# A hybrid of window attention and mixture-of-experts attention: another order of all engines, and matmuls that nobody reads in the first part

## The chip, the cores and the metric

The kernel runs on 1 core of one Trainium2 chip. The metric is the device time in microseconds; the time of the kernel before is the median of 3 runs. TensorE (PE) multiplies into PSUM, VectorE (DVE), ScalarE (ACT) and GpSimd (POOL) do the rest, and SyncE (SP) issues nearly all DMAs. Each engine takes its instructions strictly in the order in which they were laid.

## The reference

```python
def _attn_ref(q, k, v):                      # q, k, v: 8 x 8 heads x 576 x 64
    scores = scale * np.matmul(q, k.transpose(0, 1, 3, 2))
    mask = (rel >= 0) & (rel < 64)           # rel = query position - key position
    attn = softmax of scores where mask
    return np.matmul(attn, v)

def _moe_ref(x, w_gate, wq, wk, wv, wo):     # x: 8 x 576 x 512, the heads side by side
    logits = x @ w_gate                      # 4 experts; the best 2 are weighted by a softmax
    for e in range(4):
        q, k, v = x @ wq[e], x @ wk[e], x @ wv[e]            # 64 wide
        a = softmax of causal scale * (q @ k.T)
        ye = a @ v @ wo[e]
        out += weight of e for each row * ye
```

## The kernel before

The work is one program of units. A unit is a Python generator that issues some instructions at each step, and the table `ORDER` lists the units' names in the order in which their next steps are issued; behind a colon stand the PSUM banks that the step takes. The order of `ORDER` is the order of every engine's queue. There is no other scheduler.

Stage 1 is the window attention, in 72 groups `g` (9 for each batch). `p` loads q and k of two pairs of heads, `h` the values into one of three `vt` tiles. `m` makes scores of two groups (L324), `q` is their softmax (L336 to L377, over VectorE, GpSimd and ScalarE), `t` transposes the probabilities by a product with `ident` (L390) and multiplies them by the triangle masks (L393), `a` multiplies them with the values (L415) and splits the result into a high and a low f16 half, `xh` and `xl` (L440, L442). All stage 1 products are fp32.

Stage 2 is the attention of the experts, by batch: `v`, `k`, `r` (the q of stage 2) are projections of `xh` and `xl` by split weights (L566 to L568), each followed by its own split (`kt`, `qt`). `x` makes scores, `y` masks them with the running minimum (L696) and takes exp (L700), `u` weights and splits them (L732 to L755), `D` transposes them by DMA (L764), `A` multiplies them with the values (L797), `o` is the output product. `g` is the gate.

`w` prepares the weights once: the largest absolute value (L257), spread over the partitions by a product with `fours` (L262), its inverse (L265, L267), and the split. `n` takes the largest absolute value of a batch's `vt` tiles (L458, 1280 columns), `M` turns it into the scale `sc` of that batch through two small products (L465, L470) and L473, L474.

At the start `f` clears a tile `px` and issues seven matmuls of it (L209) that nobody reads. In the last batch `IDLE` puts such matmuls between the products of `A`.

Of the kernel before, what the change touches and what calls it, by code (L numbers as in the profile page):

```python
# [143 lines left out]
def window_attention_moe_attention(ctx: ExitStack, tc: tile.TileContext, qT, kT, vW,  # L144
# [10 lines left out]
    def bank():  # L155
        return PS[:, banks.pop(0)]
# [339 lines left out]
    M2 = {}  # L496
# [312 lines left out]
    def s2_o(b, j):  # L809
# [20 lines left out]
        else:  # L830
            for i in range(2):
                (nc.scalar if ends and i else nc.sync).dma_start(out[b - 1 + i, 512:576], t[64 * i:64 * i + 64])


    units = {}

    def unit(name, f, *args):
# [107 lines left out]
```

## Time and profile before

| | |
|---|---|
| median of 3 runs | 438.84 us (436.96 to 441.39) |
| time of the profiled execution | 440.07 us |
| its span | 438.4 us |
| mean granted clock of TensorE | 0.978 |
| PE busy | 390.5 us (89%), 5885 matmul records |
| DVE busy | 343.1 us (78%) |
| ACT busy | 327.4 us (75%) |
| POOL busy | 299.1 us (68%) |
| DMA moved | 71.79 MB, mean 164 GB/s |

The span is the time from the first to the last instruction of the profiled execution. An engine is busy while one of its instructions runs; a matmul's end is modelled, and matmuls overlap. Idle time of TensorE is shown with what ended it. One fp32 matmul of L209, L262, L324 or L415 leaves two records.

### The profile page before, as it was taken

What the parts mean: (1) busy time and instruction counts of PE and PEld (TensorE: products, weight loads), DVE (VectorE), ACT (ScalarE), POOL (GpSimd) and SP (SyncE); (2) the same over time, 40 slices, a digit from 0 to 9 for tenths busy, and PEclk for the clock granted to TensorE, in tenths of its full rate; (3) what the DMA queues carried; (4) which work ended last, traced back from release to release, by engine and by line L of the source; (5) the groups of instructions that cost most, each with busy time, mean ns of one, the idle gap of its engine ahead of it and who ended that gap; (6) DMA issues with size and microseconds to landing.
All of it is one profiled execution on the core that took longest, in us unless ns stands there. A gap on an engine that the chain in (4) does not pass through costs nothing. (4 is left out here: it accounts for less than half of the span.)

```text
span 438.4 us, 15501 instructions
## 1 busy us (share of the span) xinstructions
PE 390.5 (89%) x5885; PEld 296.4 (68%) x5885; DVE 343.1 (78%) x1043; ACT 327.4 (75%) x1143; POOL 299.1 (68%) x669
## 2 busy tenths in 40 slices
PE   4567998997989899999989989999999999989885
PEld 4556777776776676776676766677767775767573
DVE  2878899979897568979869877888878777878830
ACT  0756657887989577885997878967888759969942
POOL 7477533598899884887878888587699866484200
PEclk9768999999999999999999999999999999999998
DMA  7950504399299993879589968986469834587993
GB/s 247 333 187 33 201 28 137 137 187 210 62 236 209 202 242 131 191 125 187 106 200 231 221 91 161 281 178 156 91 126 203 117 63 114 116 161 128 192 229 102
DMA packets 145114, 71.79 MB, mean 164 GB/s; under 512 B 126224, under 2 KB 128784, under 8 KB 145040
## 3 DMA queue, kind: packets, MB, share of 16 engines
q1 hardware_dynamic: 144960, 70.68, 72.9%
q8 instruction: 46, 0.75, 0.8%
q14 instruction: 28, 0.23, 0.2%
q10 hardware_dynamic: 80, 0.13, 0.1%
HBM read 30.94 MB, written 9.44 MB: 92 GB/s over the span
## 5 line engine op out<-in xcount | busy, mean ns | idle before, releaser
L755 POOL TENSOR_TENSOR sp<-p,sp 128x320 f16<-128x320 f32 (+3 forms) x110 | 100.7, 915 | 9.2
L700 ACT ACTIVATE p<-p,r 128x320 f32<-128x320 f32 (+3 forms) x128 | 77.4, 609 | 16.2 <-DVE r L696 15.6
L744 ACT ACTIVATE sp<-p,r 128x192 f16<-128x192 f32 (+3 forms) x128 | 76.5, 616 | 1.8 <-DVE r L736 1.3
L754 POOL TENSOR_SCALAR p<-p,r 128x320 f32<-128x320 f32 (+3 forms) x110 | 64.5, 586 | 17.9 <-ACT sp L744 16.1
L352 ACT ACTIVATE p<-ps,st 128x64 f32<-128x64 f32 x204 | 61.4, 318 | 13.1 <-POOL st L349 11.8
L696 DVE CUSTOM_DVE_ANT_0 p<-ps,causal,sc 128x320 f32<-128x320 f32 (+2 forms) x128 | 63.6, 543 | 2.3 <-PE ps L685 1.9
L324 PE MATMUL ps<-k,q 64*64 64x128 f32 (+1 forms) x1152 | 45.1, 290 | 7.0 <-DMA k<-in_kT_dram 3.5
L377 POOL TENSOR_TENSOR p<-p,st 128x256 f32<-128x256 f32 x72 | 43.4, 614 | 8.3 <-DVE st L373 3.8
L393 DVE TENSOR_TENSOR pt<-ps,tri 128x1024 f32<-128x1024 f32 (+1 forms) x40 | 44.2, 1109 | 3.6 <-PE ps L390 3.3
L797 PE MATMUL ps<-tu,v 128*64 128x64 f16 (+2 forms) x1056 | 41.2, 229 | 5.4 <-DMA tu<-sp 2.7
L324 PEld LDWEIGHTS ps<-k,q 64*64 64x64 f32 x1152 | 36.9, 146 | 13.2 <-issue 3.2
L797 PEld LDWEIGHTS <-v 128*64 128x64 f16 x1056 | 37.4, 111 | 10.1 <-issue 8.1
L352 ACT ACTIVATION_READ_ACCUMULATOR p<-ps,st 128x1 f32 x204 | 43.0, 211 | 0.0
L685 PE MATMUL ps<-kt,qt 64*128 64x320 f16 (+3 forms) x480 | 39.8, 292 | 3.4 <-DVE pt L393 0.9
L415 PE MATMUL ps<-pt,vt 64*64 64x128 f32 (+1 forms) x1440 | 40.9, 250 | 1.8 <-DVE xl L442 0.7
L415 PEld LDWEIGHTS ps<-pt,vt 64*64 64x64 f32 x1440 | 36.3, 134 | 7.3 <-issue 1.6
L566 PE MATMUL ps<-xh,wkhi 128*128 128x256 f16 (+1 forms) x128 | 36.6, 286 | 2.9 <-DVE sc L473 1.8
L566 PE MATMUL ps<-xh,wqhi 128*128 128x256 f16 (+1 forms) x128 | 36.6, 286 | 1.6 <-ACT p L352 0.7
L566 PE MATMUL ps<-wvhi,xh 128*128 128x260 f16 x128 | 35.5, 277 | 2.0 <-DVE pt L393 1.4
L567 PE MATMUL ps<-xl,wkhi 128*128 128x256 f16 (+1 forms) x128 | 36.6, 286 | 0.2 <-DVE xl L442 0.2
L568 PE MATMUL ps<-xh,wqlo 128*128 128x256 f16 (+1 forms) x128 | 36.6, 286 | 0.0
L567 PE MATMUL ps<-xl,wqhi 128*128 128x256 f16 (+1 forms) x128 | 36.6, 286 | 0.0
(152 smaller groups left out, 1002.2 us busy)
## 6 DMA issues: line engine op xcount, KB each, us to landing
vt<-in_vW_dram SPq DMA_DIRECT2D x16, 576.0 KB, 5.5
out_dram<-out SPq DMA_DIRECT2D x32, 256.0 KB, 3.1
q<-in_qT_dram SPq DMA_DIRECT2D x14, 576.0 KB, 4.6
k<-in_kT_dram SPq DMA_DIRECT2D x14, 576.0 KB, 6.2
tu<-sp SPq DMA_TRANSPOSE x96, 3.9
out_dram<-out SPq DMA_DIRECT2D x7, 128.0 KB, 2.8
q<-in_qT_dram SPq DMA_DIRECT2D x2, 320.0 KB, 7.3
k<-in_kT_dram SPq DMA_DIRECT2D x2, 320.0 KB, 7.0
```

The costliest lines, as they stand in the source:

```text
L324: nc.tensor.matmul(S1[g][o:o + 64, i, c:], lhsT=q_t[r, i % 2, 64 * b:64 * b + 64], rhs=k_t[r, i % 2, 64 * b + c - 64:64 * b + 64], start=T ...
L352: nc.scalar.activation(pt[:, i], ps[:, i, 64:128], AF.Exp, bias=st[:, 0, z + i:z + i + 1], scale=0.125, accum_out=st[:, 1, z + i:z + i + 1])
L393: nc.vector.tensor_tensor(t, ps[:, :, None].to_broadcast([128, n, 2, 128]), tri[:, None].to_broadcast([128, n, 2, 128]), op=OP.mult)
L415: nc.tensor.matmul(to, lhsT=values[d][r, h, b + e - (w == 0)], rhs=rhs, start=(e, h) not in started, stop=s == n - 1, skip_group_check=True)
L566: nc.tensor.matmul(ps, lhsT=ah, rhs=bh, start=first, stop=False)
L567: nc.tensor.matmul(ps, lhsT=ah, rhs=bl, start=False, stop=False)
L696: nc.vector.tensor_tensor_reduce(out=dst, in0=src, in1=mask, scale=SC[b][:, 3:4], scalar=above, op0=OP.add, op1=OP.min, accum_out=to)
L700: nc.scalar.activation(p, p, AF.Exp, bias=r2[:, 0, x:x + 1], scale=-1.0, accum_out=r2[:, 1, x:x + 1])
L744: nc.scalar.activation(hi, p, AF.Copy, scale=by)
L754: nc.gpsimd.tensor_scalar(p, p, by, 1.0, op0=OP.mult, op1=OP.mult)
L755: nc.gpsimd.tensor_tensor(lo, p, hi, op=OP.subtract)
L797: nc.tensor.matmul(to, lhsT=V2[b % 2][:, c, a, 2 * pr + h], rhs=rhs, start=n == 0, stop=n == len(work_list) - 1, skip_group_check=True)
```

## The change

`ORDER` is replaced as a whole. It has the same units and steps, in another order and with other banks, and seven new ones named `F`. The durations by which the new order was laid were measured for each kind of instruction; they don't stand in the kernel. A unit `F<a or b><n>_<count>` issues `count` fp32 matmuls of 128x128 by 128 columns into a bank that the order gives it, with `px` (a) or `ident` (b) as both operands; nobody reads the result.

```diff
 ORDER = (
-    'c p0 h0 e0 p1 f:0 i h1 l0 l1 p0 n0 p1 d e1 l2 z l3 m0:01 h2 m2:23 q0 q1 q0 q3 q0 q1 q0 q2 q1 n0 q1 q1 q0 w0 q1 '
...
+    'i h0 f:0 c p0 p1 l0 h1 l1 p0 z p1 n0 l2 l3 Fa0_13:1 m0:01 h2 m2:23 q0 d q1 e1 q0 e0 q3 q0 q1 q0 w0 q1 q0 q1 q2 '
+    'Fb1_9:4 w0:0 q1 n0 q1 q1 q2 q1 q3 w0 q1 w0 Fb2_8:4 t1:0 n0 q3 w1 q2 M0:1 q2 w0 M0 Fb3_3:4 w1:4 t1 q3 M0 m8:5 q3 '
...
+    def keep_busy(n, of):
+        ps = bank()[:, :128]
+        for _ in range(n):
+            nc.tensor.matmul(ps, lhsT=of, rhs=of, start=True, stop=True)
...
             x, _, y = x.partition(":")
+            if x[0] == "F":
+                unit(x, keep_busy, int(x[1:].split("_")[1]), PX[0].rearrange("r a c -> r (a c)") if x[1] == "a" else ident)
             banks[:] = map(int, y)
             next(units[x], None)
```

The counts are 13, 9, 8, 3, 6, 3 and 4, 46 in all; the last stands ahead of t3. All other lines move down by one, so that L390 is L391 after the change.

Three places follow. The first is TensorE's queue from the weight factors of `v` (L262) to the scores m8. Before:

```order
L262 MATMUL ps<-largest,fours 128x1 x2
L390 MATMUL ps<-ident,p_0_253 128x128 x2
L390 MATMUL ps<-ident,p_1_257 128x128 x2
L465 MATMUL ps<-ident,mv_187 1x128
L262 MATMUL ps<-largest,fours 128x1
L470 MATMUL ps<-m_0_304,one 128x1
L324 MATMUL ps<-k_137,q_136 64x128 x4
```

And the same part of TensorE's queue now; L839 is the new line:

```order
L839 MATMUL ps<-ident 128x128 x9
L263 MATMUL ps<-largest,fours 128x1 x2
L839 MATMUL ps<-ident 128x128 x8
L391 MATMUL ps<-ident,p_0_265 128x128 x2
L391 MATMUL ps<-ident,p_1_270 128x128 x2
L466 MATMUL ps<-ident,mv_204 1x128
L839 MATMUL ps<-ident 128x128 x3
L263 MATMUL ps<-largest,fours 128x1
L471 MATMUL ps<-m_0_334,one 128x1
L325 MATMUL ps<-k_172,q_171 64x128 x4
```

The work that is read stands in the same order; 9, 8 and 3 unread matmuls stand ahead of the factors of `v`, of t1 and of the factor of `k`. The other 13 of the start stand right behind the seven of L209, and 6, 3 and 4 follow behind the scores.

The second place is VectorE's queue around the scale of batch 2 (`sc_1581`, from M2) and the maximum over the values of batch 3 (`mv_1563`, from n3). Before:

```order
L592 SCALAR_TENSOR_TENSOR v_1_113<-ps,v_1_113 128x256
L458 TENSOR_REDUCE mv_1563<-vt_84 128x1
L592 SCALAR_TENSOR_TENSOR v_0_114<-ps,v_0_114 64x256
L473 TENSOR_SCALAR sc_1581<-ps 128x1
L474 RECIPROCAL sc_1581<-sc_1581 128x1
```

The same place of VectorE's queue now, where the scale is called `sc_1591` and the maximum `mv_1611`:

```order
L474 TENSOR_SCALAR sc_1591<-ps 128x1
L475 RECIPROCAL sc_1591<-sc_1591 128x1
L340 COPY_PREDICATED ps<-win,ps 128x4x64
L459 TENSOR_REDUCE mv_1611<-vt_84 128x1
L807 SCALAR_TENSOR_TENSOR y_105<-ps,y_105 128x320
L593 SCALAR_TENSOR_TENSOR v_1_113<-ps,v_1_113 128x256
L652 SCALAR_TENSOR_TENSOR qt_103<-ps,qt_103 128x256
```

The scale stood behind the maximum and now stands ahead of it; a y part, a value part and a query part stand behind it.

The third place is VectorE's queue around the first maximum of batch 4 (`mv_2477`, over `vt_86`) and the second half of the keys `kt_116` of batch 2. Before:

```order
L651 SCALAR_TENSOR_TENSOR kt_115<-ps,kt_115 128x256
L651 SCALAR_TENSOR_TENSOR qt_103<-ps,qt_103 128x256
L458 TENSOR_REDUCE mv_2477<-vt_86 128x1
L393 TENSOR_TENSOR pt_30_2497<-ps,tri 128x1024
L347 TENSOR_REDUCE st_33_2516<-ps 128x4
L651 SCALAR_TENSOR_TENSOR kt_116<-ps,kt_116 128x256
```

The same place of VectorE's queue now, where the maximum is called `mv_2667`:

```order
L394 TENSOR_TENSOR pt_30_2652<-ps,tri 128x1024
L652 SCALAR_TENSOR_TENSOR kt_116<-ps,kt_116 128x256
L459 TENSOR_REDUCE mv_2667<-vt_86 128x1
L652 SCALAR_TENSOR_TENSOR qt_104<-ps,qt_104 128x320
L348 TENSOR_REDUCE st_33_2611<-ps 128x4
```

The triangle multiply and the keys stood behind the maximum and now stand ahead of it.

## Rows read from the trace of the kernel before

**Rows 1.** Busy us by stretch: length, PE, PEld, DVE, ACT, POOL, clock, DMA.
```profile
9.50:45.00 35.50, 24.63 (x396) 21.32 (x399) 27.31 (x61) 20.54 (x91) 22.48 (x40) 0.76 0.54 185
45.00:100.00 55.00, 51.33 (x826) 39.55 (x823) 50.39 (x140) 40.81 (x168) 30.59 (x80) 1.00 0.53 146
100.00:420.00 320.00, 298.38 (x4525) 223.28 (x4525) 260.40 (x827) 261.38 (x875) 238.26 (x507) 1.00 0.80 162
```

**Rows 2.** Longest waits of PE, 45 to 420 us: total, times, longest.
```profile
PE ps L566 <- DVE sc L473: 1.8, 1, 1.8
PE ps L324 <- DVE kt L651: 1.5, 1, 1.5
PE ps L390 <- DVE v L592: 1.4, 1, 1.4
```

**Rows 3.** The stretch view again, in windows of 2 us (clock third from the end).
```profile
14.00:16.00 2.00, 0.00 (x0) 0.00 (x0) 2.00 (x2) 1.69 (x12) 0.20 (x1) 0.98 1.08 367
...
24.00:26.00 2.00, 2.00 (x44) 2.00 (x40) 1.47 (x5) 0.00 (x0) 0.23 (x2) 0.50 0.00 0
...
28.00:30.00 2.00, 0.35 (x2) 0.30 (x2) 2.00 (x2) 1.86 (x13) 1.73 (x5) 0.89 1.02 369
...
32.00:34.00 2.00, 1.27 (x28) 1.30 (x30) 2.00 (x4) 2.00 (x9) 1.82 (x3) 0.50 0.87 326
```

**Rows 4.** PE's timeline, 0 to 47 us: start, us, what, [idle before <- releaser].
```profile
3.20 3.36 PE L209 MATMUL ps<-px 128*128 128x128 f32 x14 [3.20 <-DVE win L203]
...
9.50 3.19 PE L324 MATMUL ps<-k,q 64*64 64x64 f32 x60 [2.54 <-DMA k<-in_kT_dram]
16.48 0.98 PE L262 MATMUL ps<-largest,fours 128*128 128x1 f32 x4 [3.79 <-DVE largest L257]
18.13 1.09 PE L390 MATMUL ps<-ident,p 128*128 128x128 f32 x4 [0.67 <-POOL st L349]
...
20.45 5.17 PE L324 MATMUL ps<-k,q 64*64 64x128 f32 x78
...
27.56 0.38 PE L262 MATMUL ps<-largest,fours 128*128 128x1 f32 x2 [0.84 <-DVE largest L257]
29.20 0.35 PE L262 MATMUL ps<-largest,fours 128*128 128x1 f32 x2 [1.26 <-DVE largest L257]
30.65 1.09 PE L390 MATMUL ps<-ident,p 128*128 128x128 f32 x4 [1.10 <-DVE inverse L265]
32.73 1.98 PE L324 MATMUL ps<-k,q 64*64 64x64 f32 x32 [0.99 <-DMA k<-in_kT_dram]
...
41.36 0.66 PE L390 MATMUL ps<-ident,p 128*128 128x128 f32 x4
...
46.25 1.10 PE L324 MATMUL ps<-k,q 64*64 64x128 f32 x32
```

**Rows 5.** Timeline of all engines, 0 to 60 us: VectorE's rows, one load issue.
```profile
0.90 0.17 DVE L533 MEMSET m_f<- 128x128 f32 x1 [0.90 <-PEq L931]
...
22.47 0.43 DVE L339 COPY_PREDICATED ps<-win,ps 128x256 f32<-128x256 uint32 x1 [1.07 <-PE ps L324]
...
24.18 0.76 DVE L339 COPY_PREDICATED ps<-win,ps 128x256 f32<-128x256 uint32 x2 [1.28 <-PE ps L324]
...
25.88 0.39 SPq L179 DMA_DIRECT2D q<-in_qT_dram  x1
25.95 0.43 DVE L339 COPY_PREDICATED ps<-win,ps 128x256 f32<-128x256 uint32 x1 [0.36 <-PE ps L324]
```

**Rows 6.** The same view at three maxima over loaded values.
```profile
98.10 1.49 DVE L458 TENSOR_REDUCE mv<-vt 128x1 f32<-128x1280 f32 x1 [1.34 <-DMA vt<-in_vW_dram]
...
149.08 1.49 DVE L458 TENSOR_REDUCE mv<-vt 128x1 f32<-128x1280 f32 x1 [1.66 <-DMA vt<-in_vW_dram]
...
337.64 1.49 DVE L458 TENSOR_REDUCE mv<-vt 128x1 f32<-128x1280 f32 x1 [0.76 <-DMA vt<-in_vW_dram]
```

**Rows 7.** One line's durations: ns min/median/max, first and last start, forms.
```profile
L393 DVE TENSOR_TENSOR pt<-ps,tri x40: 681/1215/1225, 19.7 to 375.2; 128x1024 f32<-128x1024 f32 x32, 128x512 f32<-128x512 f32 x8
```

194 rows, old and new, of the table ORDER are left out of this document.

## Prediction

> **What bounds the kernel now.** I read four views in turn. The busy time by stretch [rows 1] shows TensorE as the engine that limits nearly all of the span: from 45 to 420 us it is busy 51.33 + 298.38 = 349.7 of 375 us, so 25.3 us idle in single pieces. VectorE is close behind from 45 to 100 us (50.39 of 55). From 9.5 to 45 us no engine is full: TensorE 24.63 and VectorE 27.31 of 35.5 us, at a mean granted clock of 0.76. That stretch is a chain of waits: first loads, scores, softmax, transposes, weight factors, then the loads of the next pairs.
>
> [...] VectorE waited for TensorE in this slow stretch [rows 5]: 1.07, 1.28 and 0.36 us for scores, while the loads of the next pairs were issued at 25.88, once the last scores of the old pairs were done.
>
> Behind 45 us the longest waits of TensorE [rows 2] are single events of 1.8, 1.5 and 1.4 us, all for VectorE. The timeline [rows 6] names what VectorE did then: it had itself waited 1.34, 1.66 and 0.76 us for a load of values (`vt`), to take that load's maximum (L458, 1.49 us). What TensorE wanted stood behind it.
>
> **Term 1, the faster clock in the first part.** Matmul counts below are records; one fp32 matmul makes two. A full-speed set of scores is 32 records in 1.10 us, 34 ns each at 46.25 [rows 4].
> - The first scores, 60 records in 3.19 us, are 53 ns each. That pace lies between 34 and the 62 ns of the set at 32.73 (1.98 us for 32), so I count them as partly slow: 60 x 19 ns = 1.1 us.
> - The transposes of t1 take 1.09 us at 18.13 and 0.66 at 41.36: 0.4 us.
> - m8, m4 and m6 (80 records) run at 5.17 us for 78, 66 ns each: 80 x 32 ns = 2.6 us. The next loads of q and k are issued when they end, so the scores at 32.73, which waited for such a load (0.99 us), move with them.
>
> Together 4.1 us. t3 (30.65) and m9 (32.73) would shrink by 0.4 and 0.9 as well; VectorE is 77% busy in this stretch and has work of its own there, so I keep that 1.3 for the upper bound, 5.4. The lower bound is nothing: if the clock is not held, or if VectorE's own queue sets the pace. I take **-4.1**.
>
> **Term 2, the unread matmuls themselves.** There are 46, each fp32 of 128x128 and 128 columns. The seven at the start took 3.36 us, 0.48 each [rows 4]. No row shows one at full clock: half of 0.48 is 0.24, and a factor matmul at about full clock, with the same weights and one column, takes 0.35 to 0.38. Thirteen stand ahead of the first scores. With the seven they last 20 x 0.48 = 9.6 us; they begin when VectorE has cleared their operand, at 3.20 before and now as VectorE's second row: its first row starts at 0.90 [rows 5], so about 1.4, an estimate. They end at 11.0 at the slow pace, 1.5 us behind the load that released the scores at 9.50, and before it if the pace doubles on the way. The other 33 cost 15.8 us slow, 12.5 at 0.38 and 7.9 at 0.24. The gaps they are to fill are 3.79 + 0.67 + 0.84 + 1.26 + 1.10 = 7.7 us [rows 4], and 4.1 more if term 1 comes true: 11.8. So at full clock they nearly fit in sum, but not gap by gap: the eight ahead of t1 (1.9 to 3.0 us) meet a gap of 0.67 plus whatever the factor matmuls come earlier. Bounds 0 and +8.2 + 1.5 = +9.7 (slow throughout). The middle of the run should be at full clock, so I take **+1.5**.
>
> **Term 3, the maxima that wait for loads.** In the old order the scale of batch 2 (L473) stood behind the maximum over `vt_84`; the new order has it ahead, and the key part `kt_116`, for which TensorE waited 1.5 us, now stands ahead of the maximum over `vt_86`. Those two stalls go, 1.8 and 1.5 us [rows 2]. At the third (1.4 us) other rows stand behind the maximum, and I can't tell. All three: 4.7. But loads and maxima are no further apart everywhere, and a y part, a value part and a query part now stand behind the two maxima. Each new wait would cost VectorE what the old ones did, 0.76 to 1.66 us, and TensorE about as much. Bounds -4.7 and 0; I take half, **-2.4**.
>
> **Term 4, the rest of TensorE's idle time.** 25.3 - 4.7 = 20.6 us in pieces of about 1 us at most. Every engine's rows move, so each piece may go or another come. For it speaks that one kind takes one time: the triangle multiply of 1024 columns is 1.22 us with median and maximum 10 ns apart [rows 7], so an order laid with measured durations can meet its waits. Against it: nothing shows that the old order's small pieces came from wrong durations. Bounds -10 (half goes) and +6 (a third more). I take a tenth, **-2.0**.
>
> **Sum.** -4.1 + 1.5 - 2.4 - 2.0 = -7.0 us. The profiled execution has a span of 438.4 and a time of 440.07 us, so about 1.7 lie around the span; the median of the three runs is 438.84 (436.96 to 441.39). Against the span that is 431.4, with what lies around it 433.1, against the median **431.8**.
>
> No load, transpose, split, bank count or tile is added or removed, so the queues' bytes are as before. On SyncE's queue the first load is now values instead of q and k; the same loads stand ahead of the second k either way, so I cost that at nothing. The unread matmuls write banks that no live tile uses, so nothing but TensorE's queue pays for them. The end (420 us on) keeps its order: the same products wait for the same transposes, and I cost it at nothing.
>
> **Rivals.**
> - **Bigger gain.** Half of TensorE's 25.3 us idle goes, because each wait was planned with the right duration: -12.6 - 4.1 + 1.5 = -15.2, 423.6 us. For: the idle pieces are small and the durations steady. Against: on the stretch from 100 to 420 all four engines are 74% to 93% busy, which leaves little to move.
> - **No change.** The clock's gain is limited to what VectorE waited for (1.07 + 1.28 + 0.36 = 2.7), the unread matmuls take 1.5 back, and the load waits only move to other maxima: -1.2, 437.6 us. For: VectorE is 92% busy from 45 to 100, so TensorE may run ahead only to wait for it.
> - **Slower: the unread matmuls stand in the way.** They are in TensorE's queue, in front of t1, the factors and the next transposes, and can't be skipped. What stands behind them is released late, and ScalarE, GpSimd and the next loads with it. Slow they cost 15.8 against 7.7 us of gaps, 8.2 too much, and 1.5 at the start; nothing of term 1 comes back. With terms 3 and 4 as taken, 438.8 + 9.7 - 4.4 = 444.1 us. It decides from 0.36 us for one on (11.8 / 33): above it the first part is longer than before. Against: 0.38 was measured with the clock only just up, and 20 in a row at the start leave TensorE busy from 1.4 us.
>
> [...]
>
> **How the numbers follow.** Likeliest (427 to 434.4): 0.42. Bigger gain (under 427): 0.18. No change (434.4 to 443.2): 0.27. [...] One per cent, 4.4 us, is about what a measurement of this kernel can tell from no change: faster 0.60, same 0.27, slower 0.13. For 8 in 10 the range takes in the bigger gain's price and stops short of the slow rival's: 423 to 443. The likeliest case alone has 427 to 434.4.
>
> **What would show it.** Term 1: a granted clock of 1.00 from about 15 to 45 us, m8, m4 and m6 at 34 ns a record, and the loads that were issued at 25.88 issued 3 to 4 us earlier. Term 2: an unread matmul at 0.24 to 0.36 us, and t1 no later than 18.1. Term 3: no wait of TensorE over 1 us for L473's or a `kt` part's sake behind a maximum; VectorE may still wait for a load; it is TensorE's waits that count. Term 4: TensorE idle under 25 us from 45 to 420. I am wrong if the clock is 1.00 and the first part still ends when it did (VectorE bound it), or if it is short and the stretch behind it has grown by as much.

## The result, and the profile after

The changed kernel takes 422.88 us (median of 4 runs, 422.35 to 423.95) beside 438.78 of the kernel before on the same chip: ratio 0.9636, 95% interval 0.9583 to 0.969, 15.9 us faster. I had forecast 431.8 and 423 to 443. The direction was right; the size was more than twice the forecast, and the time lies just outside the range. Its profiled execution has a span of 420.8 us.

The busy time by stretch, as in [rows 1], then the stretch from 145 to 390 us by itself (columns as there; the clock is third from the end):
```profile
9.50:45.00 35.50, 30.19 (x569) 25.73 (x573) 31.62 (x75) 25.19 (x112) 26.33 (x48) 1.00 0.62 220
45.00:100.00 55.00, 50.31 (x782) 39.71 (x774) 48.25 (x139) 38.76 (x150) 31.19 (x75) 1.00 0.57 146
100.00:420.00 320.00, 304.99 (x4593) 228.43 (x4591) 258.83 (x824) 264.83 (x881) 233.79 (x501) 0.99 0.81 168
...
145.00:390.00 245.00, 241.61 (x3698) 182.40 (x3696) 211.22 (x667) 212.02 (x716) 195.50 (x416) 1.00 0.83 169
```
The kernel before in that last stretch:
```profile
145.00:390.00 245.00, 229.34 (x3499) 172.10 (x3499) 195.82 (x612) 195.77 (x672) 187.21 (x406) 1.00 0.79 162
```
Here lies most of the gain: TensorE's idle time falls from 15.7 to 3.4 us, and in the same 245 us it issues 3698 matmul records for 3499, 5.7% more. The first part runs at a clock of 1.00 for 0.76, and from 45 to 100 us TensorE is no busier than before.

TensorE's timeline of the first part, as in [rows 4]:
```profile
1.39 3.36 PE L210 MATMUL ps<-px 128*128 128x128 f32 x14 [1.39 <-DVE px L203]
4.54 3.99 PE L839 MATMUL ps<-px 128*128 128x128 f32 x26
...
9.63 1.76 PE L325 MATMUL ps<-k,q 64*64 64x64 f32 x60 [0.83 <-DMA k<-in_kT_dram]
11.32 2.27 PE L839 MATMUL ps<-ident 128*128 128x128 f32 x18
...
16.73 0.68 PE L391 MATMUL ps<-ident,p 128*128 128x128 f32 x4 [0.38 <-DVE inverse L266]
...
18.73 2.84 PE L325 MATMUL ps<-k,q 64*64 64x128 f32 x80
...
29.22 1.10 PE L325 MATMUL ps<-k,q 64*64 64x64 f32 x32
...
33.03 1.20 PE L325 MATMUL ps<-k,q 64*64 64x128 f32 x32 [1.09 <-DVE pt L394]
...
36.10 1.13 PE L416 MATMUL ps<-pt,vt 64*64 64x64 f32 x48 [1.19 <-DVE p L360]
...
38.67 0.41 PE L391 MATMUL ps<-ident,p 128*128 128x128 f32 x2 [1.44 <-DVE pt L394]
```
L839 are the unread matmuls, two records each: 3.99 / 13 = 0.31 us, later 2.27 / 9 = 0.25. m8, m4 and m6 (18.73) take 35 ns a record for 66. From 33 us on TensorE waits for VectorE.

The table compares places rather than times. Every step of TensorE is weighed with the time that a step of its kind takes in before when nothing holds it up (unread matmuls count nothing), and the sums are lined up: how many us earlier than in before a kernel has done the same work. The columns are times of before. Each row is one execution beside one execution of before, which was itself 1.3 us over its median; so the last column lies above what the medians say (2.2 for 0.4 in old_maxima). In kernels that equal before up to there, or all but, the entry differs from 0 by up to 2.5, so that much is chance. The kernels are told of below; "old" begins from the order of before, "new" from that of after. The median of old_pe leaves out one run that was over 1.5% longer than its fastest.

| kernel | 37 | 92 | 148 | 237 | 325 | 413 | 430 | median us | ratio to before, 95% |
|---|---|---|---|---|---|---|---|---|---|
| after | 6.5 | 3.2 | 3.0 | 7.2 | 14.2 | 21.8 | 17.5 | 422.88 | 0.9636 [0.9583, 0.969] |
| new_no_unread | 0.7 | -4.3 | -3.2 | -0.4 | 5.8 | 13.8 | 9.2 | 426.03 | 0.9741 [0.9677, 0.9804] |
| old_unread | -2.5 | -2.6 | -2.7 | -3.5 | -4.3 | -4.0 | -3.4 | 444.32 | 1.0153 [1.0105, 1.0201] |
| old_unread2 | 3.4 | 3.3 | 3.2 | 2.3 | 1.5 | 2.1 | 2.7 | 438.57 | 1.0003 [0.9976, 1.003] |
| old700_new | 0.6 | -1.0 | -5.9 | -1.1 | 5.9 | 14.2 | 9.0 | 430.28 | 0.9799 [0.9735, 0.9864] |
| new710_old | 6.6 | 3.4 | -0.1 | -6.3 | -7.2 | -6.7 | -6.1 | 444.98 | 1.0145 [1.0104, 1.0186] |
| old_maxima | 1.3 | 0.8 | 0.7 | 1.5 | 1.4 | 2.0 | 2.2 | 437.65 | 0.999 [0.9966, 1.0015] |
| old_banks | 1.0 | -1.3 | -4.7 | -13.7 | -20.1 | -24.0 | -24.1 | 463.19 | 1.0563 [1.0519, 1.0607] |
| old_banks2 | 1.1 | 0.8 | 0.9 | 1.1 | 1.3 | 1.8 | 1.6 | 438.17 | 0.9994 [0.9966, 1.0021] |
| new_banks | 6.5 | 3.1 | 3.1 | 7.1 | 15.7 | 24.4 | 19.1 | 421.42 | 0.9617 [0.9572, 0.9663] |
| old_v | 0.4 | -0.5 | -6.4 | -4.8 | -4.7 | -5.9 | -9.1 | 450.39 | 1.0267 [1.0194, 1.0341] |
| old_pe | 0.0 | 0.0 | -2.8 | -12.3 | -19.3 | -25.1 | -24.7 | 464.58 | 1.0546 [1.0431, 1.066] |
| new_all | 6.5 | 1.1 | -5.6 | -14.0 | -11.5 | -8.4 | -17.6 | 458.44 | 1.0438 [1.0375, 1.0501] |
| old_v2 | 2.5 | 1.6 | 0.8 | -0.2 | 0.8 | 2.7 | -0.3 | 437.32 | 0.9946 [0.9919, 0.9973] |
| old_pe2 | 0.4 | -1.0 | -2.2 | -4.5 | -6.4 | -4.2 | -4.5 | 443.71 | 1.009 [1.006, 1.012] |
| old_all2 | 1.2 | 0.2 | 2.4 | 5.7 | 8.2 | 14.8 | 13.6 | 427.16 | 0.9737 [0.971, 0.9763] |
| new_all2 | 7.0 | 4.5 | 5.5 | 8.8 | 13.6 | 20.8 | 16.0 | 424.51 | 0.9655 [0.9606, 0.9704] |
| new_tail | 6.1 | 3.0 | 2.8 | 7.0 | 15.6 | 22.4 | 19.9 | 422.42 | 0.9624 [0.9584, 0.9664] |

So after gains 6.5 us up to 37, loses 3.5 of them up to 148, gains 18.8 up to 413, and gives 4.3 back at the end.

The loss up to 148 has two places. By the same sums 2 us are gone by 45 us, where TensorE waits for VectorE. Some 3 more go between 110 and 130, where after's clock falls again, from 119 us on, behind idle pieces of 0.99, 0.74 and 0.20 us in which TensorE waited for VectorE:
```profile
116.55 0.58 PE L686 MATMUL ps<-kt,qt 64*128 64x320 f16 x6 [0.99 <-DVE r L697]
117.88 0.74 PE L686 MATMUL ps<-kt,qt 64*128 64x448 f16 x6 [0.74 <-DVE m L697]
```
```profile
118.00:120.00 2.00, 1.80 (x34) 1.30 (x32) 2.00 (x9) 2.00 (x8) 1.92 (x3) 0.78 1.07 121
120.00:122.00 2.00, 2.00 (x48) 2.00 (x43) 1.73 (x5) 1.19 (x6) 1.75 (x4) 0.50 1.42 126
```

### The profile page after: what moved, and what is told of

Its sections match the earlier page's. It is cut to its first block, busy times and chain, and to the rows that moved or that the text cites. A ratio compares the mean times of both kernels' runs of the same rounds, so it can differ in the third digit from the quotient of the medians.

```text
span 420.8 us, 15689 instructions
## 1 busy us (share of the span) xinstructions
PE 392.9 (93%) x5977; PEld 301.0 (72%) x5977; DVE 342.7 (81%) x1043; ACT 328.8 (78%) x1143; POOL 299.1 (71%) x669
## 5 line engine op out<-in xcount | busy, mean ns | idle before, releaser
L755 POOL TENSOR_SCALAR p<-p,r 128x320 f32<-128x320 f32 (+3 forms) x110 | 64.6, 587 | 22.1 <-ACT sp L745 15.7
L745 ACT ACTIVATE sp<-p,r 128x320 f16<-128x320 f32 (+3 forms) x128 | 75.8, 613 | 0.9 <-POOL r L737 0.3
L378 POOL TENSOR_TENSOR p<-p,st 128x256 f32<-128x256 f32 x72 | 43.3, 616 | 14.3 <-DVE st L374 13.5
L798 PE MATMUL ps<-tu,v 128*64 128x256 f16 (+2 forms) x1056 | 41.5, 230 | 3.7 <-DVE y L807 1.7
L325 PE MATMUL ps<-k,q 64*64 64x128 f32 (+1 forms) x1152 | 39.9, 271 | 3.4 <-DVE r L697 1.2
L416 PE MATMUL ps<-pt,vt 64*64 64x128 f32 (+1 forms) x1440 | 39.4, 252 | 2.4 <-DVE p L360 1.2
L416 PEld LDWEIGHTS ps<-pt,vt 64*64 64x64 f32 x1440 | 35.3, 136 | 7.7 <-issue 2.7
L325 PEld LDWEIGHTS ps<-k,q 64*64 64x64 f32 x1152 | 32.6, 134 | 8.5 <-DVE r L697 2.4
L569 PE MATMUL ps<-xh,wklo 128*128 128x256 f16 (+1 forms) x128 | 36.6, 286 | 0.0
```

Of the source, the lines that this page charges most:

```text
L325: nc.tensor.matmul(S1[g][o:o + 64, i, c:], lhsT=q_t[r, i % 2, 64 * b:64 * b + 64], rhs=k_t[r, i % 2, 64 * b + c - 64:64 * b + 64], start=T ...
L416: nc.tensor.matmul(to, lhsT=values[d][r, h, b + e - (w == 0)], rhs=rhs, start=(e, h) not in started, stop=s == n - 1, skip_group_check=True)
L569: nc.tensor.matmul(ps, lhsT=al, rhs=bh, start=False, stop=last)
L745: nc.scalar.activation(hi, p, AF.Copy, scale=by)
L755: nc.gpsimd.tensor_scalar(p, p, by, 1.0, op0=OP.mult, op1=OP.mult)
L798: nc.tensor.matmul(to, lhsT=V2[b % 2][:, c, a, 2 * pr + h], rhs=rhs, start=n == 0, stop=n == len(work_list) - 1, skip_group_check=True)
```

## Experiments on the first part: the unread matmuls

All edits are to `ORDER`. In new_no_unread the seven entries are taken out of after; in old_unread they are put into before at the same places.
```diff
-... Fa0_13:1 m0:01 ... Fb1_9:4 w0:0 ...      after
+... m0:01 ... w0:0 ...                       new_no_unread
...
-... m0:01 ... w0:0 ...                       before
+... Fa0_13:0 m0:01 ... Fb1_9:0 w0:0 ...      old_unread
+... Fa0_13:6 m0:01 ... Fb1_9:7 w0:0 ...      old_unread2
```
new_no_unread: 

> The changed kernel without the 46 unread matmuls. Theory of the prediction: the clock falls again between 15 and 36 us, terms 1 and 2 are lost together (4.1 - 1.5), 425.5 us. Rival 'the gain is in the order behind 145 us': the lead at 145 us is 3.0 us, so at most 426, and 422.5 to 423.5 if the order alone made that lead. If the unread matmuls carried most of the gain: 432 or more.

It is 3.1 us slower than after (426.03), or 4.2 where each is set against the runs of before on its own chip. The sign agrees with the 2.6 of terms 1 and 2; the size is uncertain, since the intervals of the two ratios overlap. This kernel's runs spread over 6.3 us (424.53 to 430.84) where after's spread over 1.6. The execution profiled here is the slowest of the four (430.84, mean granted clock 0.956); the other three took 424.53 to 426.41 at 0.979 to 0.987, and after's four had 0.987 to 0.991. So this trace, and its row in the table, overstate what the unread matmuls are worth. Its clock, by stretch:
```profile
14.00:16.00 2.00, 0.97 (x4) 0.93 (x4) 2.00 (x4) 1.48 (x11) 0.25 (x2) 0.50 1.08 366
24.00:26.00 2.00, 1.66 (x30) 1.26 (x22) 2.00 (x5) 0.76 (x5) 0.70 (x3) 0.55 0.00 0
```
old_unread: 

> The order and the banks of before with the 46 unread matmuls put in at the same seven places (ahead of the first scores, of the factors of v, of t1, of the factors of k, q and o, and of t3). Theory of the prediction: 438.8 - 4.1 + 1.5 = 436.2 us. Rival 'they stand in the way': 440 or more. If they carried most of the gain: 430 or less.

A miss by 8 us; the rival came true. The timeline shows why:
```profile
15.58 4.18 PE L840 MATMUL ps<-ident 128*128 128x128 f32 x18 [3.67 <-ACT p L354]
19.55 0.85 PE L264 MATMUL ps<-largest,fours 128*128 128x1 f32 x4
...
24.55 0.86 PE L392 MATMUL ps<-ident,p 128*128 128x128 f32 x4
```
I had given the nine unread matmuls the bank of the step behind them. They waited 3.67 us for ScalarE, its last reader, filled no gap, and ran at the slow pace (0.46 us each) in front of the factors; t1 came at 24.55 for 18.13. In after they go to banks that nobody reads at that time. So they do in the next kernel.

old_unread2: 

> Before with the 46 unread matmuls at the same seven places as in old_unread, but in banks that nobody reads at that time, so that they need not wait. Prediction's terms 1 and 2: -4.1 + 1.5 = -2.6, 436.2 us; with the bounds of term 2 from 434 to 447. Rival (in the old order they stand in the way even so): over 440, as old_unread's 444.3. Sign of the first: the 78 records of m8, m4 and m6 at 34 to 36 ns each and begun before 20.45; of the second: t1 later than 18.13.


```profile
9.50:45.00 35.50, 29.61 (x557) 25.85 (x557) 28.48 (x68) 23.25 (x102) 24.47 (x45) 1.00 0.54 185
```
```profile
12.46 2.28 PE L840 MATMUL ps<-ident 128*128 128x128 f32 x18
16.89 0.58 PE L264 MATMUL ps<-largest,fours 128*128 128x1 f32 x4 [2.15 <-DVE largest L259]
...
19.19 0.60 PE L392 MATMUL ps<-ident,p 128*128 128x128 f32 x4
...
20.93 2.73 PE L326 MATMUL ps<-k,q 64*64 64x128 f32 x78
```
Full clock throughout, 35 ns a record, t1 1 us late, and 3.4 us ahead at 37 in this trace; the medians show no difference (1.0003, so within about 1.3 us either way). Of the first sign the pace came true and the start did not (20.93, not before 20.45); the second sign came true. The steps in the chain (weight maxima, factors) wait for VectorE, 2.15 us ahead of the first factor, at a clock of 1.00 too. From old_unread to old_unread2 only four bank numbers of unread matmuls differ: 5.8 us, and 1.5% by the ratios.

The executions of before say the same. In the 70 that stand beside these runs the mean granted clock lies anywhere from 0.970 to 0.992. The 19 with 0.985 or more are not faster (in the median 0.3 us above the median of their chip) than the 42 under 0.98 (0.1 below it). So in the old order the time does not hang on the mean clock. The clock of [rows 3] was that of one execution: in old700_new below, whose first part is that of before, it is 0.90 from 9.5 to 45 us for 0.76.

## Experiments on the middle: which part of the order

**Splices.** Up to about 145 us one order, behind it the other.
```diff
+... x113:51 y112 u101 k200 v22:7 | y113 q32 k200 u100 ...       old700_new: before | after
+... q32 u110 A100:2 o03 y112 o02 | u101 u101 u101 u101 D1020 ... new710_old: after | before
```
old700_new: 

> The order of before for its first 700 entries (to about 145 us), then all other steps in the order of the changed kernel, without unread matmuls. Rival 'the gain is in the order behind 145 us': the lead grows from 3.0 to 21.8 us between 145 and 391 us and falls to 17.5 at the end, so 438.8 - 14.5 = 424 us (422 to 428). Theory of the prediction: terms 1 and 2 lost, half of terms 3 and 4 lost, 436 us (434 to 438).

new710_old: 

> The first 710 entries of after's order with the unread matmuls (to about 145 us), then the rest as before has it. Read from the two traces the first part is about 3 us ahead at 145 us and the rest gains 18.8 us up to 391 us and gives 4.3 back. If the gain of the middle is made by the middle's own order, this kernel keeps 2 to 5 us: 434 to 437. If it comes from the clock and the lead of the first part (whatever is ahead stays ahead and grows), it is near after: 422 to 428. The prediction's terms 1 and 2 alone give 436.2.

The join costs each some 5 us of waits (one of 4.3 us in the first, of 3.6 and 1.9 in the second). Behind it the table is plain: from 148 to 413 the new order gains 20.1 us behind the old first part, and the old order gains nothing behind the new one (-6.3 at 237, -6.7 at 413). The busy time from 160 to 390 us says it without the table (before, old700_new, new710_old):
```profile
160.00:390.00 230.00, 216.33 (x3318) 161.54 (x3317) 186.18 (x584) 186.31 (x634) 174.06 (x380) 1.00 0.76 157
```
```profile
160.00:390.00 230.00, 227.78 (x3527) 172.27 (x3526) 198.77 (x627) 200.98 (x689) 186.09 (x400) 1.00 0.81 169
```
```profile
160.00:390.00 230.00, 215.74 (x3313) 159.78 (x3306) 184.61 (x579) 185.42 (x635) 171.97 (x372) 0.99 0.75 155
```
The middle's gain belongs to the middle's own order; neither clock nor lead is needed for it. The time of old700_new, 7.4 us better than before, lies between the two forecasts for that reason: the join and the end take back 11 of the 20.

**The three maxima (term 3).**
```diff
-... A000:3 v04 n3 q25 ... | ... u110 u110 n4 t30:2 k211 ... | ... q68 u501 n7 q68 ...
+... A000 M2 n3 k101:5 ... | ... q33 k211 n4 q34 ...         | ... q68 q67 n7 v62 ...
```
old_maxima: 

> Before with three maxima moved back behind the split that they held up (n3 behind M2's last step, the first half of n4 behind k211's split, the second half of n7 behind t66): term 3 of the prediction alone. Prediction: 2.4 us faster, 436.4 (at most 4.7, 434.1). Rival: the three waits move to the next bank or operand, and the time is that of before, 438 to 439.5.

Near the rival's number: 437.65, ratio 0.999. TensorE's waits move on. What the maxima took in the old order was not 2.4 us: the interval ends at 1.5.

**Banks.** With each step of TensorE matched to the last reader of its bank, 23.0 of the 23.1 us for which TensorE stood idle ahead of a step in before behind 45 us (pieces over 0.05 us) end when its bank comes free, and in about 19 of them another bank was free. That looks like a bad choice of banks.
```diff
-... m9:20 ... v00:1 ... t8:1 ... a10:34 ...
+... m9:21 ... v00:0 ... t8:2 ... a10:27 ...      old_banks
+... m9:21 ... v00:0 ... t8:2 ... a10:12 ...      old_banks2
```
old_banks: 

> The order of before, step for step, with other PSUM banks only: each step gets the bank whose last reader was done earliest in the trace of before (357 of the choices differ). From 45 us on, TensorE's stalls over 0.05 us sum to 23.1 us in the trace of before, and 23.0 of it ended when the bank that the step was given had been read out by VectorE or ScalarE; in 19.5 us of it another bank lay empty at the stall's start. Theory of the prediction (clock, loads, small pieces): banks don't matter, 436 to 441 us. Rival 'banks chosen badly': 420 to 430 us. Rival 'banks released late, whichever is chosen' (the readers stand late in their queues): 434 to 440 us.

None of these. `a` is read with one access pattern over both its banks; in before they are always neighbours, and I had put 31 of 40 pairs apart. TensorE's waits from 145 to 413 us:
```profile
PE ps L567 <- DVE xl L443: 7.0, 6, 1.9
PE ps L686 <- DVE xl L443: 2.4, 2, 1.3
PE ps L325 <- DVE xl L443: 1.8, 2, 1.0
PE ps L568 <- DVE xl L443: 1.6, 2, 1.3
PE ps L798 <- DVE xl L443: 1.5, 2, 1.3
```
L443 is the second reader of `a`. Of the 15.0 us for which TensorE waited for it (14.3 in these lines) 13 were spent ahead of steps whose banks the pattern does not touch; nearly all of those banks lie between its two. I read this as waits of the program that cover all that lies between the first and the last bank of the pattern; no run shows it by itself. old_banks2 keeps the pairs together.

old_banks2: 

> The order of before on every engine, only the numbers of the PSUM banks chosen anew (180 of the bank numbers differ), so that each TensorE step gets the bank that was released longest before it in the trace of before; the two banks of an `a` step stay neighbours, which old_banks had broken in 31 of 40 places. In the trace of before 23.0 us of TensorE's stalls after 45 us ended with the release of the step's bank, and in 19.5 us of them another bank was free when the stall began. Theory banks (the middle's gain is a better choice of banks): 15 to 20 us faster than before, 419 to 424. Theory order (what counts is that ScalarE, VectorE and GpSimd read the banks and prepare the operands earlier): a stall that loses its bank finds the next wait, for an operand or for the next bank, and 0 to 5 us are gained, 434 to 439.

new_banks: 

> The order of after on every engine with bank numbers chosen anew in the same way from the trace of after (162 differ). There 13.7 us of TensorE's stalls after 45 us ended with a bank's release, 8.3 of them with another bank free. Theory banks: 5 to 8 us faster than after, 415 to 418. Theory order: within 3 us of after, 420 to 424.

The waits for `xl` shrink from 15.0 to 1.6 us (the longest wait is now 1.5 us, for a transpose), TensorE's idle time ahead of steps behind 45 us falls from 23.1 to 14.3, and the time does not move: 438.17, ratio 0.9994. What was idle time ahead of a step became time within steps (x steps above all, 0.57 us for 0.50, waiting for their second bank or operand); counted over all matmuls, TensorE's idle pieces fall only from 26.3 to 25.7 us. In after new banks give 1.5 us, within the noise. The stalls of before are for banks (23.0 of 23.1 us), yet another choice of banks did not help. That all of them come free at the pace of their readers is how I read it; no run shows it by itself.

**Which engines.** Here the queues are laid anew by a search that plays them through with each instruction's duration from the two traces. In old_v2 only VectorE, ScalarE and GpSimd change, in old_pe2 only TensorE and its banks, in old_all2 both. A piece of VectorE's queue (step.number) in old_v2, and of TensorE's in old_pe2:
```diff
-v42.3 r400.3 q52.7 q53.2 q54.2 q53.3 g40.1 M5.2 v43.3 y313.1 y400.1 M5.4
+r400.3 v42.3 q53.2 q53.3 g40.1 M5.2 y313.1 M5.4 q54.2 g40.3 n6.1 y400.1
...
-A300.1 A310.1 m55.1 o30.1 r411.1 x410.1 x403.1 o31.1 t53.1 t52.1 A311.1 a53.1
+A310.1 A300.1 x402.1 r411.1 x410.1 o30.1 m55.1 o31.1 t53.1 x414.1 t52.1 A311.1
```
The first attempt (old_v, old_pe, and new_all from after's order) had wrong durations. All the kernels laid in this way, which are those from here on, have one more difference: VectorE clears `px` first of all, so that the first unread matmuls begin at 1.12 us where before's begin at 3.20 and after's at 1.39.

old_v: 

> TensorE's order, its PSUM banks, and SP's order are word for word those of before; only the queues of VectorE, ScalarE and GpSimd are laid anew from about 100 us on (452 of 713, 331 of 572 and 260 of 426 entries stand elsewhere, by two places on average), with each instruction's duration taken from the two traces. What TensorE waits for is then the only thing that changes. Theory readers (the middle's 17 us of the change come from VectorE, ScalarE and GpSimd standing ready in the order in which TensorE asks): 10 to 30 us faster than before, 408 to 428. Theory TensorE (the gain is TensorE taking another step while one is blocked): at most 4 us faster, 434 to 439, as its order is the old one. Prediction's term 4 gave 2 us for everything of this kind.

old_pe: 

> The mirror image of old_v: the queues of VectorE, ScalarE, GpSimd and SP are those of before, and only TensorE's order (214 of 386 steps stand elsewhere, by one place on average) and the numbers of its banks (219) are laid anew from about 100 us on, with the same durations. In the trace of before TensorE stood idle for 17.7 us between 145 and 413 us, and in 13.8 us of them another of its next steps had its inputs. Theory TensorE: 8 to 14 us faster than before, 424 to 430. Theory readers: at most 8 us faster, 430 to 439, less than old_v gains.

new_all: 

> After, with its unread matmuls and its order up to 46 us, and from there on TensorE, its banks, VectorE, ScalarE and GpSimd laid anew once more in the same way (262, 555, 447 and 307 entries stand elsewhere; SP as in after). If the queues' order with measured durations is what the time hangs on, there is more to have than after took: after's TensorE is busy for 392.9 us of 420.8, and in-step waits are a part of that; 395 to 415. If after has reached what the order can give (busy 93%), 418 to 424.

All three miss, 12 to 26 us slower than before (new_all 36 slower than after). In an `x` step two matmuls start together and the next pair follows some 0.2 us later (at 385.67, 385.87 and 386.06 us in the step of after below); I had counted nearly every start as 0.004 us. In after's timeline such a step of 448 columns takes
```profile
385.67 0.74 PE L686 MATMUL ps<-kt,qt 64*128 64x448 f16 x6
```
and by my durations 0.37. Transposes by DMA had a fixed 3.3 us from issue to landing; in before they take 3.0 to 6.4, median 4.0, between 100 and 390 us. new_all, laid for transposes that always land in 3.3 us, waited for them (100 to 390 us):
```profile
PE ps L799 <- DMA tu<-sp: 6.7, 2, 5.5
```
With both mended, by the same search (with a slower set of durations averaged in as a margin):

old_v2: 

> As old_v (TensorE's and SP's order and the banks word for word those of before; VectorE 505 of 713, ScalarE 378 of 572, GpSimd 308 of 426 entries stand elsewhere, by two places on average), but laid with mended durations: TensorE's steps with the start to start time of each of their matmuls, and DMA transfers that queue behind one another as in the traces. Theory readers: 12 to 20 us faster than before, 419 to 427, most of what the middle of after gained. Theory joint (TensorE's order and the readers' have to fit each other, neither alone gives it): within 6 us of before, 433 to 439. old_v, the same edit with wrong durations, took 450.4.

old_pe2: 

> As old_pe (only TensorE's order, 180 of 386 steps by one place on average, and 210 bank numbers; all other queues as before), with the mended durations. Theory readers: 0 to 6 us faster than before, 433 to 439, clearly less than old_v2. Theory TensorE: more than old_v2 gains, under 425. old_pe, with wrong durations, took 465.4.

old_all2: 

> Before with TensorE's order (205 of 386 steps elsewhere), its banks (198) and the queues of VectorE (494 of 713), ScalarE (390 of 572) and GpSimd (288 of 426) laid anew together from about 75 us on, with the mended durations of old_v2 and old_pe2; SP's order and the first part as before, no unread matmuls. Theory joint (the queues have to fit each other): 12 to 22 us faster than before, 417 to 427, where old_v2 gained 2.4 and old_pe2 lost 4. Theory additive (each engine's part adds up): 2.4 less 4, near 440. Theory SP (without SP's new order nothing can be had): 434 to 440.

new_all2: 

> As new_all (after up to 46 us with its unread matmuls, then TensorE, banks, VectorE, ScalarE and GpSimd laid anew; SP as in after), with the mended durations. If the durations are what the order hangs on, the kernel is faster than after: 402 to 415. If after has what can be had, 420 to 426. new_all, with wrong durations, took 458.4.

Stretch 145 to 390 us of old_v2, old_pe2 and old_all2, to set beside the two at the top:
```profile
145.00:390.00 245.00, 231.34 (x3515) 174.11 (x3512) 198.38 (x616) 199.64 (x678) 188.58 (x407) 0.99 0.76 160
```
```profile
145.00:390.00 245.00, 231.18 (x3492) 169.29 (x3487) 193.44 (x602) 195.10 (x673) 186.33 (x398) 1.00 0.77 159
```
```profile
145.00:390.00 245.00, 239.22 (x3619) 176.54 (x3616) 205.71 (x648) 206.40 (x702) 194.90 (x418) 1.00 0.82 166
```
The readers alone give 2.2 us, TensorE alone loses 4.2, both together gain 11.7. It is the joint order: the effects don't add. (Each was laid by a search of its own, so old_all2 is not the sum of the other two edits.) The theory of the readers, which I held after the banks, fell with old_v2. In old_v2 TensorE waited 5.2 us for transposes in this stretch (longest 2.0), where before waited 1.3; I read this as readers that finish sooner and meet a TensorE that still asks in the old order, which no run shows by itself. new_all against new_all2, 458.4 against 424.5, has the durations as its main difference: 34 us; the margin came with them, and its share is not known. New_all2 is not faster than after; there TensorE is busy 242.7 of 245 us, so idle time leaves little more to gain.

**The end.**
```profile
401.29 0.71 PE L798 MATMUL ps<-tu,v 128*64 128x256 f16 x20 [1.73 <-DVE y L807]
402.95 0.69 PE L798 MATMUL ps<-tu,v 128*64 128x256 f16 x10 [0.95 <-DMA tu<-sp]
403.58 0.61 PE L567 MATMUL ps<-wohi,y 128*128 128x512 f16 x1
...
406.19 0.38 PE L568 MATMUL ps<-wolo,y 128*128 128x512 f16 x1
```
After's end has two new waits, and behind them the clock falls: 0.61 us for an output matmul of 0.38.
```profile
404.00:406.00 2.00, 2.00 (x7) 0.76 (x6) 0.49 (x1) 0.12 (x1) 0.00 (x0) 0.54 1.03 198
```
```diff
-... new_banks up to about 380 us | its last steps
+... new_banks up to about 380 us | 17 TensorE steps, 68 VectorE and 19 SP entries elsewhere
```
new_tail: 

> new_banks (after with its banks chosen anew, 421.4) with the last stretch, from about 380 us on, laid anew: 17 of TensorE's steps, 68 entries of VectorE, 44 of ScalarE and 19 of SP stand elsewhere. After is 21.8 us ahead of before at 391 us and 17.5 at the end: 4.3 us are given back there, 2.7 of them in two waits of the steps A710 at 401 and 403 us. If these hang on the order of the last steps: 2 to 4 us faster than new_banks, 417 to 419. If the last chain (transposes, products, output, one behind the other) sets the end whatever the order: within 1 us of new_banks, 420.5 to 422.5.

422.42, no gain over new_banks. TensorE now waits 3.7 us in five pieces for transposes instead. That the chain of transposes, products and output sets the end whatever the order is not refuted, but one other order is no proof of it. No version beat after by more than the measurement tells.

## Why the prediction was right and wrong

- **Term 1 (-4.1): the durations came as priced.** m8, m4 and m6 at 35 ns a record (2.3 us less), the first scores 1.76 for 3.19 (1.4), t1 0.68 for 1.09 (0.4): 4.1. The clock was 1.00 from 9.5 to 45 us, the loads of 25.88 were issued from 21.61 on. t3 and m9 shrank too (0.63 for 1.09, 1.10 for 1.98). That the unread matmuls would hold the clock was my estimate; in the profiled executions it is 1.00 in after and old_unread2 and 0.86 in old_unread, where they waited for a bank, and without them 0.64 (new_no_unread), 0.76 (before) and 0.90 (old700_new). That shorter steps shorten the kernel is borne out for the new order only, and only together with term 2 (new_no_unread); in the old order the same clock gives nothing in the medians (old_unread2).
- **Term 2 (+1.5): right as the price of one**, 0.25 to 0.31 us each, t1 at 16.73; what all 46 cost was not measured by itself. Both terms together were forecast at -2.6; the lead at 148 us is 3.0, and taking them out of after costs about 3.1. That the sum fits so well is in part luck, since it hides two movements: 6.5 ahead at 37 us, more than forecast, and 3.5 given back up to 148. TensorE waits for VectorE (1.09, 1.19 and 1.44 at 33 to 39 us, 0.99 and 0.74 ahead of the slow clock at 119). That is what the rival "no change" said of VectorE, in part.
- **Term 3 (-2.4): the mechanism came, the size did not.** No wait of TensorE over 1 us for L473 or a `kt` part is left from 45 to 420 us (the longest is 0.9). With the three maxima moved alone in the old order the time falls by 0.4 us (interval -1.5 to +0.7). The step that failed: I priced a stall by its length, as if nothing stood behind it.
- **Term 4 (-2.0, bounds -10 and +6): this step failed.** With term 3 I forecast -4.4 for all behind the first part; from 148 to 413 the lead grew by 18.8. Two errors. The larger is the share: I took a tenth of the idle time because "nothing shows that the old order's small pieces came from wrong durations", with half as the bound, and from 145 to 390 us nearly four fifths of it went (15.7 to 3.4 us). The other is what I left out: I counted only idle time, and TensorE also loses time within steps. Measured against steps that nothing holds up, some 40 us were lost from 148 to 413 in the old order and some 22 in the new one; idle time ahead of steps was 16 to 17 of the first and 3 to 4 of the second, so about 13 of the gain is idle time and 5 lies within steps. Orders laid with wrong durations turned out 13 to 34 us worse than with mended ones, so durations matter to an order as the argument for this term had it. That the old order's own pieces came from wrong durations no run shows.
- **The end (0): wrong by 4.3 us**: 2.7 in the two waits at 401 and 403 us, and about 1 in the output matmuls at the slow clock behind them.
- **Sum by the traces:** -3.0 - 18.8 + 4.3 = -17.5, against 438.4 - 420.8 = 17.6 of the two spans. The medians differ by 15.9: the profiled execution of before lies 1.3 us over its median, that of after 0.4 under.
- **Rivals.** "Bigger gain" (423.6, chance 0.18) is what happened, in time and in the idle share that went (12.6 priced, 12.3 from 145 to 390 us); old_all2 bears out waits planned together, while the right durations as their reason are shown only for orders laid anew here. The chance was too small, as I argued from busy shares of 74% to 93% that little could move; TensorE went from 94% to 99% from 145 to 390 us. "Slower" did not come, since its price of 0.36 us was not reached; old_unread shows that it is real where an unread matmul has to wait for its bank. The mean clock differs from execution to execution in before (0.970 to 0.992) and in new_no_unread (0.956 to 0.987); after holds it in all four runs (0.987 to 0.991), which lie within 1.6 us, so "slower" did not come in a part of its runs either.

What stays open: which pairs of queues have to fit, and what makes the time within steps. SP's order was never changed alone: old_all2, which keeps it, gains 12.4 us from 148 to 413 where after gains 18.8, and whether SP or a better search makes the rest is not known.

## What to carry to other kernels

With the four engines 68% to 89% busy and a table that sets their queues, the small waits of the bound engine were one thing here, not many: taking away the longest ones, choosing better buffers for them, or mending one side's queue gave from 2 us to a loss of 4, and mending all queues together 12 (old_all2) and 19 (the middle of after). Price such a change by the whole loss of the bound engine, between steps and within them, and test the durations first: the tables laid with wrong ones were 12 to 36 us slower than the orders that they replaced. Give an unread matmul a bank whose readers are long done: in old_unread nine of them waited 3.67 us for theirs, and the kernel took 444.32 us for 438.57 in old_unread2. A faster clock did not shorten the old order (old_unread2: 1.00 from 9.5 to 45 us for 0.76, ratio 1.0003); read the clock over several executions, not one.

## What had not been expected of the hardware

- Where one reading pattern took two banks apart from each other (old_banks), TensorE waited 13 us for it ahead of steps in other banks, nearly all of them between the two; with the two as neighbours (old_banks2) 0.2 us.
- The clock fell in after behind pieces of 1.73 and 0.95 us idle (0.60 from 402 to 404 us, 0.54 from 404 to 406), and output matmuls took 0.61 to 0.63 us for 0.38 until 405.7 us. It fell at 119 us too, behind pieces of 0.99, 0.74 and 0.20 us (0.50 from 120 to 122).
- The mean granted clock of one and the same kernel differs from execution to execution: 0.970 to 0.992 in before, with no gain in time at the upper end.
- Four bank numbers of unread matmuls were worth 5.8 us (444.32 to 438.57).
